# Where the gate product, the next token tile's split and the weight conversion stand in a fused attention and two-layer MoE kernel

## The chip, the cores and the metric

The kernel runs on one core of one Trainium2 chip. The metric is the device time of one execution in microseconds (us). Three executions of the kernel before took 931.65, 932.81 and 933.22 us; the median is 932.81 us.

## The reference, cut to what matters

```python
# q, k, v: (4, 8, 576, 64)
kv  = einsum('bhsd,bhse->bhde', k, v)
o   = einsum('bhsd,bhde->bhse', q, kv)
x   = o / sqrt(mean(o*o, -1) + 1e-6) * g_norm      # to (2304 tokens, 512)
y   = (sigmoid(x @ w_gate) * (x @ w_val)) @ w_out  # 512 -> 1536 -> 512
out = softplus(y @ w_in2) @ w_out2                 # 512 -> 2048 -> 512
```

All is fp32. The kernel reaches that accuracy by splitting both operands of a product into a rounded part (HI) and a rest (LO) and adding three fp32r matmuls: HI by HI, HI by LO, LO by HI, with the weight first. So a product needs the LO half of its weight at its third matmul and the LO half of the data at its second.

## The kernel before, in words

**Order.** The program is written out by hand. Each engine works through its own queue in the order in which the Python code emits instructions, so the place of a call in the loop is its place in the queues of PE (TensorE), ACT (ScalarE), DVE (VectorE) and SP (DMA issue).

**Tiles and iterations.** The first layer has five token tiles (512, 512, 384, 384, 512 tokens) and 12 blocks of 128 hidden columns: 60 iterations n = (t, i). One iteration has three groups of 12 matmuls: `ffn1_mm` "g" (PSUM tile ps_g), `ffn1_mm` "v" (ps_v) and `ffn1_out` of the iteration before it (yacc). The second layer follows with 80 iterations (ps_h, oacc). ps_g and ps_v share the pool `mm`, which has two buffers. So the v product of iteration n+1 can only start when `gated` of iteration n has read ps_v, and the g product of n+1 when `sigmoid` of n has read ps_g.

**After the products.** `sigmoid` (L488, ACT) writes sg. `gated` multiplies sg by ps_v (L494, DVE) and rounds the result into ghl HI (L67, ACT); `gated_lo` writes ghl LO (L70, DVE). Before the change `gate_prev` and `gate_lo_prev` call these for the previous iteration, after the g product of this one.

**Weights.** Weights arrive as raw fp64 words in 18 items of 1 MB for the first layer, each with a block of SBUF of its own, and 16 for the second. Item numbers go gate/value 0, gate/value 1, out 0 and 1, gate/value 2, gate/value 3, out 2 and 3, and so on: iteration 1 needs item 1 for g and v and item 2 for its out product, iteration 2 needs item 3, iteration 3 items 4 and 5. An item is converted on the chip: `conv_a` (two ACT instructions, L141 and L143), `conv_b` (two DVE, L150 and L153), `conv_h` (one ACT, L67) and `conv_l` (one DVE, L70). `conv_step` makes one step of each for successive items; `conv_to(m)` repeats it until m items are done. `A_LIM` and `L_END` say how far it goes in each iteration; the steps of an iteration are spread over three places.

**Attention.** Token tile 0 is prepared before the loop (L370 transposes it, `xt_split` at L381 and L382 splits it), interleaved with the first three quarters of g(0) and the conversion of weight 0 in two halves (`early_*`). Tile 1 is prepared during iterations 2 to 8 of the loop: `kv_mm` (L258), `qt_mm` (L320), `o_mm` (L332), `o_scale` (L364), `xt_mm` (L370). Later tiles come during the tile ahead of them, in 28 pieces of one head pair: `q_trans` (transpose L422, then the split of hl), `po_mm`, `po_evac`, `ss_mm`, `rms_root`, `rms_scale`. A table of places says where: "A", "B", "C" are slots behind the g, v and out products on PE, and "a", "b", "c", "bg" and "late" the matching slots for ACT and DVE.

**Scratch.** Before the loop the last seven weight blocks hold attention data (k, v, q rows, squares, the output rows `ON`). Their weight loads come when the data is used up.

```python
    def mm3(ps, lhs, rhs, start, stop):                    # L63
        for n, (a, b) in enumerate(PASSES): ...
    def gated(t, i):
        nc.vector.tensor_tensor(out=sg, in0=sg, in1=chain.pop(("v", t, i)), op=ALU.mult)   # L494
        split_hi(ghl[:, HI], sg)                           # L67
    def conv_step():
        na, nb = n_a[0], n_b[0]
        if n_h[0] < nb: conv_h()
        if na < min(n_load[0], a_lim[0]): conv_a()
        if nb < na: conv_b()
        if n_l[0] < n_h[0]: conv_l()
    def x_split(u):                                        # x: one buffer for all tiles
        for hp in range(NP):
            split(x_tile(u)[:, hp, HI, :n], x_t[u][:, hp, LO, :n], of_t[u][:, hp, :n])
```

Of the kernel before, what the change touches and what calls it, by code (L numbers as in the profile page):

```python
# [29 lines left out]
def attention_moe_moe_kernel(ctx: ExitStack, tc: tile.TileContext, q, k, v, g_norm,  # L30
                             w_gate, w_val, w_out, w_in2, w_out2, out):
    nc = tc.nc
# [4 lines left out]
    P = 128  # L37
# [172 lines left out]

    SCR = [n for n in range(n_first - 7, n_first)]
    KV, QROWS, QT, SQ, KVF, ON = 0, 5, (7, 8), 9, 10, (12, 13)
    scr_t = {}

    def scratch(gen, j, name):
# [94 lines left out]
    def half(u, j, hp, name):  # L312
        return scratch(u, j, name)[:, hp % 2 * 512:(hp % 2 + 1) * 512]
# [25 lines left out]
    def o_square(u, hp):  # L339
# [5 lines left out]
        nc.scalar.activation(out=sq, in_=ps, func=ACTF.Square)  # L345
        nc.vector.tensor_reduce(out=ms_t[u, 0][:, hp], in_=heads(sq), op=ALU.add, axis=AXIS.X)

    def on_rows(u, hp):
        return half(u, ON[hp // 2], hp, "on").rearrange("p (n m) -> p n m", m=P)


    def o_keep(u, hp):
# [13 lines left out]
    def xt_mm(u, hp, pool):  # L366
        ps = pool[0].tile([P, 512], F32, tag=pool[1], name="xT")
        on = on_rows(u, hp)
        for n in range(NS):
            nc.tensor.transpose(ps[:, n * P:(n + 1) * P], on[:, n], ident)  # L370
        at_ps["xT", u, hp] = ps
# [275 lines left out]
    def early_l(j):  # L647
        split_lo(early["w"][:, j, LO], early[j][:, :, 0].bitcast(F32), early["w"][:, j, HI])
# [66 lines left out]
    xt_mm(0, 2, ACC)  # L715
    a_root(3)
    a_scale(3)
    nc.scalar.preload_act_table_set("sigmoid_and_others")
    xt_split(0, 2)
    ffn1_mm(0, 0, "g", (1,))  # L720
    early_b(1)
    xt_mm(0, 3, ACC)
    early_h(1)
    xt_split(0, 3)
    early_l(1)
    ffn1_mm(0, 0, "g", (2,))
    a_lim[0] = 2
    conv_a()
    conv_b()
    for part in (0, 1, 2, 3, "rest"):  # L730
        load_kv(1, part)
# [20 lines left out]
    def at_mm(places, mm_fs, evac_fs):  # L752
        for (n, c), f, g in zip(places, mm_fs, evac_fs):
# [1 line left out]
            at_place(n, c.lower(), g)  # L755

    hps = range(NP)
    at_mm(((2, "A"), (2, "B"), (2, "C"), (3, "A")), [call(kv_mm, 1, h) for h in hps], [call(kv_evac, 1, h) for h in hps])
    at_mm(((3, "B"), (3, "C"), (4, "A"), (4, "B")), [call(qt_mm, 1, h, ATP) for h in hps],
          [call(qt_evac, 1, h) for h in hps])  # L760
    at_mm(((4, "C"), (5, "A"), (5, "B"), (5, "C")), [call(o_mm, 1, h, ATP) for h in hps],
          [lambda h=h: (o_square(1, h), o_keep(1, h)) for h in hps])
    at_place(6, "bg", call(o_root, 1, slice(0, NP)))
    at_place(6, "late", call(o_scale, 1, 0), call(o_scale, 1, 1))
    at_place(7, "bg", call(o_scale, 1, 2), call(o_scale, 1, 3))
    at_place(7, "late", call(kvb_split))
    at_mm(((7, "A"), (7, "B"), (7, "C"), (8, "A")), [call(xt_mm, 1, h, ATP) for h in hps],
          [call(xt_keep, 1, h) for h in hps])
    for n, c, m in ((3, "late", 2), (4, "late", 1), (5, "late", 2), (8, "bg", 2)):
        at_place(n, c, *[load_item] * m)  # L770

    for u in range(2, NT1):
        j = (u - 1) * F1 + (0 if u > 2 else 1)
        ps = pieces(u)
        for n, p in enumerate(ps):
            b, m = p[0], p[3]
            if (b > ps[n - 1][0] if n else b > (TILES1[u][0] - 1) // S):
                at_place(j - 1, "bg", call(load_kv, b, "rest"), call(load_kv, b, 0), call(load_kv, b, 1))
                for part, c in ((2, "b"), (3, "c")):
                    at_place(j, c, call(load_kv, b, part))  # L780
                for hp, (d, c) in enumerate(((0, "B"), (0, "C"), (1, "A"), (1, "B"))):
                    at_place(j + d, c, call(kv_mm, b, hp))
                    work[j + d, c.lower()] = [call(kv_evac, b, hp)] + work.get((j + d, c.lower()), [])
                j += 2
            at_place(j - 1, "bg", call(load_q, u, p))
            step = 2 if m <= 160 else 1
            for h0 in range(0, NP, step):
                hh = range(h0, h0 + step)
                at_place(j, "a", *[call(q_trans, u, p, h) for h in hh])
                at_place(j, "B", *[call(po_mm, u, p, h) for h in hh])  # L790
                at_place(j, "b", *[call(po_evac, u, p, h) for h in hh])
                j += 1
                at_place(j, "A", *[call(ss_mm, u, p, h) for h in hh])
                at_place(j, "a", *[call(ss_evac, u, p, h) for h in hh])
            at_place(j, "bg", call(rms_root, u, p))
            if n + 1 < len(ps) and TILES1[u - 1][1] < 512 and m > 160:
                when = ((1, "bg"), (2, "bg"), (3, "bg"), (4, "bg"))
            else:
                when = ((1, "bg"), (1, "late"), (2, "bg"), (2, "late"))
            for h, (d, c) in enumerate(when):  # L800
                at_place(j + d, c, call(rms_scale, u, p, slice(h, h + 1)))
            if u == 3 and n == 0:
                j += 1


    A_LIM = (4, 6, 7, 9, 10, 12, 13, 15, 16, 18, 18, 18)
    L_END = (3, 5, 6, 8, 9, 11, 12, 14, 15, 17, 18, 18)

    def conv_target(n):
        i = n - (n1 - F1)  # L810
# [13 lines left out]
    for n in range(len(its) + LAG2):  # L824
        ph, t, i = its[n] if n < len(its) else (0, 0, 0)
        prev = its[n - 1] if 0 < n <= len(its) else (0, 0, 0)

        def run(place):
            for f in work.pop((n, place), ()):
                f()  # L830

        def gate_prev():
            if prev[0] == 1:
                gated(*prev[1:])

        def gate_lo_prev():
            if prev[0] == 1:
                gated_lo(*prev[1:])

        if ph == 1:  # L840
            done = n_l[0]
            step = max(0, conv_target(n) - done)
            ffn1_mm(t, i, "g", range(3 if n == 0 else 0, KD))
            run("A")
            gate_prev()
            run("a")
            gate_lo_prev()
            if n:
                conv_to(done + (step + 2) // 3)
            sigmoid(t, i)  # L850
            run("bg")
            if t == NT1 - 1 and i < 2:
                y_split(0, 2 * i)
                y_split(0, 2 * i + 1)
            ffn1_mm(t, i, "v")
            run("B")
            conv_to(done + (2 * step + 2) // 3)
            run("b")
            conv_to(done + step)
        elif ph == 2:  # L860
            if n == n1:
                gate_prev()
                gate_lo_prev()
                xs.close()
                g2pool = ctx.enter_context(tc.tile_pool(name="g2pool", bufs=3))
                epool = ctx.enter_context(tc.tile_pool(name="epool", bufs=2))
                nc.scalar.preload_act_table_set("natural_log_exp_and_others")
            ffn2_mm(t, i)
            if prev[0] == 2:
                soft_sum(*prev[1:])  # L870
            if n_l[0] < len(items) and i % 2 == 0:
                a_lim[0] = len(items)
                conv_step()
            if t + 1 < NT2:
                if i == 10:
                    y_load(t + 1)
                if F2 - KD <= i:
                    y_split(t + 1, i - F2 + KD)
            soft_exp(t, i)
            if prev[0] == 2:  # L880
                soft_hi(*prev[1:])
            soft_ln(t, i)
            if prev[0] == 2:
                soft_lo(*prev[1:])
        elif n == len(its):
            soft_sum(*prev[1:])
            soft_hi(*prev[1:])
            soft_lo(*prev[1:])
        if prev[0] == 1:
            ffn1_out(*prev[1:])  # L890
        if n >= LAG2 and its[n - LAG2][0] == 2:
            ffn2_out(*its[n - LAG2][1:])
        run("C")
        run("c")
        run("late")
        if ph == 1 and t == NT1 - 1:
            n_free[0] = i + 1 + i // 2
            prefetch()
        if ph == 1 and i == F1 - 1 and t + 1 < NT1:
            x_split(t + 1)  # L900
            if t + 1 == NT1 - 1:
                at.close()
                y0pool = ctx.enter_context(tc.tile_pool(name="y0pool", bufs=1, side="right"))
        if ph == 1 and t == NT1 - 2 and i == F1 - 3:
            y_load(0)
# [31 lines left out]
```

## Time and profile before

| what | value |
|---|---|
| median of three executions | 932.81 us |
| the profiled execution's own time | 931.42 us |
| span of its instructions | 929.6 us |
| mean granted TensorE clock | 0.992 of full speed |
| PE busy | 907.6 us, 98% |
| DVE busy | 548.4 us, 59% |
| ACT busy | 457.3 us, 49% |

Times in the trace count from the start of the span. The profiled execution is 1.8 us longer than its span and 1.4 us shorter than the median. A bracket behind a row of a timeline gives the time for which the engine stood idle ahead of it and what ended that. Instructions that follow one another on an engine overlap a little in the record, so a sum over rows uses the distance of their starts.

### The profile page before, as it was taken

To read this page: it belongs to the slowest core of one execution; us is meant where nothing else is said; L and a number is where in the kernel's file an instruction comes from. 1 tells how busy PE (TensorE), PEld (TensorE's weight loads), DVE (VectorE), ACT (ScalarE), POOL (GpSimd) and SP (SyncE) were. 2 spreads that over 40 slices of the span, in tenths; PEclk is the share of its full clock that TensorE was granted. 3 is DMA by queue.
4 is the path that set the end of the run, shared out by engine and by line. 5 is a ranking of instruction groups with operands and counts; after the bars stand their busy time and mean duration, and the time that the engine had idled before them with its cause. 6 is when DMAs were issued, how large, how long until landed. Compare 5 with 4: busy or idle time off the path is not lost.

```text
span 929.6 us, 11913 instructions
## 1 busy us (share of the span) xinstructions
PE 907.6 (98%) x4653; PEld 780.9 (84%) x4653; DVE 548.4 (59%) x908; ACT 457.3 (49%) x791; POOL 1.6 (0%) x8
## 2 busy tenths in 40 slices
PE   8699989999999999999999999999999999999998
PEld 6477778878899999999888878888888999888886
DVE  4755784343555534575475688765556666566554
ACT  4646773332345343543565576554454454555443
POOL 0000000000000000000000000000000000000000
PEclk9799999999999999999999999999999999999999
DMA  9982130330011302002556301011002002000001
GB/s 307 281 285 95 51 103 0 103 76 7 1 57 52 78 6 71 10 24 61 200 195 212 110 27 46 1 42 38 1 1 80 1 1 81 1 0 35 1 1 45
DMA packets 73960, 64.73 MB, mean 70 GB/s; under 512 B 33200, under 2 KB 64944, under 8 KB 73904
## 3 DMA queue, kind: packets, MB, share of 16 engines
q1 hardware_dynamic: 72672, 63.33, 21.8%
q10 hardware_dynamic: 1232, 0.66, 0.3%
q8 instruction: 36, 0.59, 0.2%
q14 instruction: 20, 0.16, 0.1%
HBM read 54.53 MB, written 9.44 MB: 69 GB/s over the span
## 4 chain that ended last, share of the span: by engine, by line
PE 88%; DVE 5%; DMA 3%; SPq 2%; issue 1%; ACT 1%
PE oacc L63 21%; PE ps_h L63 21%; PE yacc L63 15%; PE ps_v L63 15%; PE ps_g L63 14%; DMA kv_raw<-in_k_dram 2%; DVE w_raw L150 1%; DVE w L70 1%; SPq L130 1%; PE kv_ps L258 1%; PE po L63 1%; DVE w L153 1%; DMA kv_raw<-in_q_dram 0%; DMA w_raw<-in_moe_w_out_dram 0%; DMA q_raw<-in_q_dram 0%
## 5 line engine op out<-in xcount | busy, mean ns | idle before, releaser
L63 PE MATMUL oacc<-w,ghl 128*128 128x512 f32 x864 | 210.7, 391 | 0.7 <-DVE ghl L70 0.7
L63 PEld LDWEIGHTS oacc<-w,ghl 128*128 128x128 f32 x864 | 161.4, 188 | 34.1 <-DVE ghl L70 1.9
L63 PE MATMUL ps_v<-x,w 128*128 128x512 f32 (+1 forms) x720 | 163.6, 376 | 8.3 <-DVE sg L494 8.2
L63 PE MATMUL ps_g<-x,w 128*128 128x512 f32 (+1 forms) x720 | 161.2, 371 | 2.9 <-ACT x L381 2.2
L63 PE MATMUL yacc<-ghl,w 128*128 128x512 f32 (+1 forms) x720 | 159.6, 370 | 0.0
L63 PEld LDWEIGHTS ps_v<-x,w 128*128 128x128 f32 x720 | 132.3, 192 | 27.6 <-DVE sg L494 10.0
L63 PEld LDWEIGHTS ps_g<-x,w 128*128 128x128 f32 x720 | 130.8, 188 | 21.9 <-ACT x L381 2.8
L63 PEld LDWEIGHTS yacc<-ghl,w 128*128 128x128 f32 x720 | 129.8, 188 | 16.6
L560 ACT ACTIVATE e<-ps_h 128x512 f32<-128x512 f32 (+1 forms) x80 | 44.4, 555 | 180.7 <-PE ps_h L63 171.5
L63 PE MATMUL ps_h<-y,w 128*128 128x512 f32 (+1 forms) x576 | 128.3, 372 | 0.0
L63 PEld LDWEIGHTS ps_h<-y,w 128*128 128x128 f32 x576 | 106.2, 188 | 16.4
L569 DVE TENSOR_SCALAR u<-e 128x512 f32<-128x512 f32 (+1 forms) x80 | 32.0, 399 | 133.1 <-ACT e L561 133.0
L67 ACT CAST ghl<-sg 128x512 fp32r<-128x512 f32 (+1 forms) x60 | 34.6, 577 | 103.2 <-DVE sg L494 103.0
L63 PE MATMUL ps_h<-y_odd,w 128*128 128x512 f32 (+1 forms) x384 | 82.4, 363 | 0.0
L63 PEld LDWEIGHTS ps_h<-y_odd,w 128*128 128x128 f32 x384 | 70.2, 188 | 8.9
L494 DVE TENSOR_TENSOR sg<-sg,ps_v 128x512 f32<-128x512 f32 (+1 forms) x60 | 37.7, 629 | 46.2 <-PE ps_v L63 44.4
L488 ACT ACTIVATE sg<-ps_g 128x512 f32<-128x512 f32 (+1 forms) x60 | 33.3, 555 | 39.5 <-PE ps_g L63 39.4
L578 DVE TENSOR_TENSOR e<-e,u 128x512 f32<-128x512 f32 (+1 forms) x80 | 51.1, 638 | 2.8
L571 DVE SCALAR_TENSOR_TENSOR e<-ps_h,e 128x512 f32<-128x512 f32 (+1 forms) x80 | 51.0, 638 | 2.8
L70 DVE TENSOR_TENSOR ghl<-sg,ghl 128x512 fp32r<-128x512 f32 (+1 forms) x60 | 38.1, 636 | 23.5 <-ACT ghl L67 23.3
L70 DVE TENSOR_TENSOR ghl<-e,ghl 128x512 fp32r<-128x512 f32 (+1 forms) x80 | 50.3, 628 | 0.7 <-ACT ghl L67 0.7
L570 ACT ACTIVATE ln<-u 128x512 f32<-128x512 f32 (+1 forms) x80 | 47.2, 591 | 6.8 <-DVE u L569 6.0
(97 smaller groups left out, 774.1 us busy)
## 6 DMA issues: line engine op xcount, KB each, us to landing
w_raw<-in_moe_w_out_dram SPq DMA_DIRECT2D x28, 512.0 KB, 4.5
w_raw<-in_moe_w_in_dram SPq DMA_DIRECT2D x16, 512.0 KB, 4.9
w_raw<-in_moe_w_gate_dram SPq DMA_DIRECT2D x12, 512.0 KB, 5.8
w_raw<-in_moe_w_val_dram SPq DMA_DIRECT2D x12, 512.0 KB, 7.5
out_dram<-ob SPq DMA_DIRECT2D x17, 256.0 KB, 2.5
kv_raw<-in_k_dram SPq DMA_DIRECT2D x16, 256.0 KB, 3.7
kv_raw<-in_v_dram SPq DMA_DIRECT2D x14, 256.0 KB, 4.0
y_dram<-ys SPq DMA_DIRECT2D x6, 512.0 KB, 2.8
```

What stands on the lines that cost most here:

```text
L63: nc.tensor.matmul(out=ps, lhsT=lhs(a), rhs=rhs(b), start=start and n == 0, stop=stop and n == 2)
L67: nc.scalar.copy(out=hi, in_=src)
L70: nc.vector.tensor_tensor(out=lo, in0=src, in1=hi.bitcast(F32), op=ALU.subtract)
L130: nc.sync.dma_start(out=t, in_=unit(w, f))
L150: nc.vector.scalar_tensor_tensor(out=lo, in0=hi, scalar=3, in1=lo, op0=ALU.logical_shift_left, op1=ALU.bitwise_or)
L488: nc.scalar.activation(out=sg, in_=chain.pop(("g", t, i)), func=ACTF.Sigmoid)
L494: nc.vector.tensor_tensor(out=sg, in0=sg, in1=chain.pop(("v", t, i)), op=ALU.mult)
L560: nc.scalar.activation(out=e, in_=ps, func=ACTF.Abs)
L569: nc.vector.tensor_scalar(out=u, in0=e, scalar1=1.0, scalar2=None, op0=ALU.add)
L570: nc.scalar.activation(out=ln, in_=u, func=ACTF.Ln)
L571: nc.vector.scalar_tensor_tensor(out=e, in0=chain.pop(("p", t, i)), scalar=0.0, in1=e, op0=ALU.max, op1=ALU.add)
L578: nc.vector.tensor_tensor(out=e, in0=e, in1=u, op=ALU.subtract)
```

## The change

The gate product of an iteration is finished in that iteration: `sigmoid` comes straight after the g product, `gated` and `gated_lo` after the v product. The conversion is spread over two places, ahead of the v product and behind `gated_lo`, and iterations 0 and 1 each finish one item fewer (`L_END`), though iteration 0 begins one step more. `x_split` of the next token tile moves ahead of `gated` in the last iteration of a tile. Before the loop the sigmoid table is loaded behind the conversion `conv_a` of item 1, which itself moves ahead of `early_l(1)`. The output rows `on` live in the tile `of`, so six scratch blocks do, item 11 is loaded before the loop, and later loads come earlier. Most places of tile 1's attention move forward by one, and so do those of `rms_scale`.

```diff
-    SCR = [n for n in range(n_first - 7, n_first)]
-    KV, QROWS, QT, SQ, KVF, ON = 0, 5, (7, 8), 9, 10, (12, 13)
+    SCR = [n for n in range(n_first - 6, n_first)]
+    KV, QROWS, QT, SQ, KVF = 0, 5, (7, 8), 9, 10
...
     def on_rows(u, hp):
-        return half(u, ON[hp // 2], hp, "on").rearrange("p (n m) -> p n m", m=P)
+        return of_tile(u)[:, hp].rearrange("p (n m) -> p n m", m=P)
...
     a_root(3)
     a_scale(3)
-    nc.scalar.preload_act_table_set("sigmoid_and_others")
     xt_split(0, 2)
     ffn1_mm(0, 0, "g", (1,))
     early_b(1)
+    a_lim[0] = 2
     xt_mm(0, 3, ACC)
     early_h(1)
     xt_split(0, 3)
+    conv_a()
     early_l(1)
     ffn1_mm(0, 0, "g", (2,))
-    a_lim[0] = 2
-    conv_a()
+    nc.scalar.preload_act_table_set("sigmoid_and_others")
     conv_b()
...
-    at_mm(((2, "A"), (2, "B"), (2, "C"), (3, "A")), [call(kv_mm, 1, h) for h in hps], ...
-    at_mm(((3, "B"), (3, "C"), (4, "A"), (4, "B")), [call(qt_mm, 1, h, ATP) for h in hps],
-    at_mm(((4, "C"), (5, "A"), (5, "B"), (5, "C")), [call(o_mm, 1, h, ATP) for h in hps],
+    at_mm(((1, "C"), (2, "A"), (2, "B"), (2, "C")), [call(kv_mm, 1, h) for h in hps], ...
+    at_mm(((3, "A"), (3, "B"), (3, "C"), (4, "A")), [call(qt_mm, 1, h, ATP) for h in hps],
+    at_mm(((4, "B"), (4, "C"), (5, "A"), (5, "B")), [call(o_mm, 1, h, ATP) for h in hps],
+    at_place(5, "late", call(kvb_split))
     at_place(6, "bg", call(o_root, 1, slice(0, NP)))
-    at_place(6, "late", call(o_scale, 1, 0), call(o_scale, 1, 1))
-    at_place(7, "bg", call(o_scale, 1, 2), call(o_scale, 1, 3))
-    at_place(7, "late", call(kvb_split))
+    at_place(6, "b", call(o_scale, 1, 0))
+    at_place(6, "c", call(o_scale, 1, 1))
+    at_place(7, "bg", call(o_scale, 1, 2))
+    at_place(7, "b", call(o_scale, 1, 3))
-    for n, c, m in ((3, "late", 2), (4, "late", 1), (5, "late", 2), (8, "bg", 2)):
+    for n, c, m in ((2, "late", 2), (3, "late", 1), (4, "late", 1), (5, "late", 1), (8, "bg", 1)):
         at_place(n, c, *[load_item] * m)
...
-                when = ((1, "bg"), (1, "late"), (2, "bg"), (2, "late"))
+                when = ((0, "late"), (1, "bg"), (1, "late"), (2, "bg"))
             for h, (d, c) in enumerate(when):
                 at_place(j + d, c, call(rms_scale, u, p, slice(h, h + 1)))
...
     A_LIM = (4, 6, 7, 9, 10, 12, 13, 15, 16, 18, 18, 18)
-    L_END = (3, 5, 6, 8, 9, 11, 12, 14, 15, 17, 18, 18)
+    L_END = (2, 4, 6, 8, 9, 11, 12, 14, 15, 17, 18, 18)
...
             ffn1_mm(t, i, "g", range(3 if n == 0 else 0, KD))
             run("A")
-            gate_prev()
+            sigmoid(t, i)
             run("a")
-            gate_lo_prev()
-            if n:
-                conv_to(done + (step + 2) // 3)
-            sigmoid(t, i)
             run("bg")
+            conv_to(done + (step + 1) // 2)
             if t == NT1 - 1 and i < 2:
                 y_split(0, 2 * i)
                 y_split(0, 2 * i + 1)
             ffn1_mm(t, i, "v")
             run("B")
-            conv_to(done + (2 * step + 2) // 3)
+            if i == F1 - 1 and t + 1 < NT1:
+                x_split(t + 1)
+            gated(t, i)
             run("b")
+            gated_lo(t, i)
             conv_to(done + step)
+            if n == 0:
+                conv_step()
         elif ph == 2:
             if n == n1:
-                gate_prev()
-                gate_lo_prev()
                 xs.close()
...
         if ph == 1 and i == F1 - 1 and t + 1 < NT1:
-            x_split(t + 1)
             if t + 1 == NT1 - 1:
```

## Rows read from the trace of the kernel before

**Rows 1.** Page, part 1: busy time, share of the span, instructions.

```profile
PE 907.6 (98%) x4653; PEld 780.9 (84%) x4653; DVE 548.4 (59%) x908; ACT 457.3 (49%) x791; POOL 1.6 (0%) x8
```

**Rows 2.** Waits of PE over the whole span: us in total, times, longest.

```profile
PE ps_v L63 <- DVE sg L494: 8.2, 4, 4.9
PE xT L370 <- DVE on L364: 2.5, 2, 1.3
```

**Rows 3.** Timeline of PE, 24 to 56 us: start, us, engine, line, operation, idle before.

```profile
24.48 0.66 PE L370 MATMUL xT<-kvf,on 128*128 128x128 f32 x4 [1.23 <-DVE on L364]
...
28.82 2.00 PE L63 MATMUL ps_g<-x,w 128*128 128x512 f32 x3 [1.85 <-ACT x L381]
30.62 4.53 PE L63 MATMUL ps_v<-x,w 128*128 128x512 f32 x12
...
43.27 5.08 PE L63 MATMUL ps_v<-x,w 128*128 128x512 f32 x12 [4.91 <-DVE sg L494]
48.19 2.91 PE L63 MATMUL yacc<-ghl,w 128*128 128x512 f32 x12
50.94 2.88 PE L63 MATMUL ps_g<-x,w 128*128 128x512 f32 x12
53.75 0.95 PE L258 MATMUL kv_ps<-kv_raw 128*64 128x64 f32 x20
54.62 3.01 PE L63 MATMUL ps_v<-x,w 128*128 128x512 f32 x12
```

**Rows 4.** Windows: busy us of PE, PEld, DVE, ACT, POOL; PE clock; DMA.

```profile
28.00:34.00 6.00, 5.18 (x11) 3.76 (x12) 3.81 (x4) 3.99 (x6) 0.00 (x0) 0.50 1.06 371
...
38.00:43.00 5.00, 0.36 (x2) 0.00 (x0) 4.97 (x5) 1.73 (x2) 0.00 (x0) 0.79 0.72 140
...
103.00:106.00 3.00, 3.00 (x14) 2.42 (x14) 1.92 (x2) 3.00 (x4) 0.00 (x0) 1.00 0.94 294
```

**Rows 5.** Timeline of ACT, 23 to 31 us.

```profile
23.41 1.28 ACT L718 ACT_TABLE_LOAD   x1
24.71 0.69 ACT L381 ACTIVATE x<-xT,g_col 128x512 fp32r<-128x512 f32 x1
...
28.67 1.15 ACT L141 ACTIVATE w_raw<-w_raw 128x1024 f32<-128x1024 f32 x1
```

**Rows 6.** Timeline of DVE, 25 to 44 us.

```profile
25.43 0.75 DVE L382 SCALAR_TENSOR_TENSOR x<-xT,g_col,x 128x512 fp32r<-128x512 f32 x1 [1.00 <-ACT x L381]
...
40.26 1.23 DVE L153 SCALAR_TENSOR_TENSOR w<-w_raw 128x1024 uint32<-128x1024 uint32 x1
41.40 1.22 DVE L70 TENSOR_TENSOR w<-w,w 128x1024 fp32r<-128x1024 f32 x1
42.54 0.68 DVE L494 TENSOR_TENSOR sg<-sg,ps_v 128x512 f32<-128x512 f32 x1
```

**Rows 7.** Groups of DVE and ACT over the span: busy us, mean ns.

```profile
L150 DVE SCALAR_TENSOR_TENSOR w_raw<-w_raw 128x1024 uint32<-128x1024 uint32 x33 | 40.3, 1220 | 3.9 <-ACT w_raw L143 3.8
...
L141 ACT ACTIVATE w_raw<-w_raw 128x1024 f32<-128x1024 f32 x33 | 38.3, 1160 | 0.0
...
L67 ACT CAST w<-w 128x1024 fp32r<-128x1024 f32 x33 | 34.5, 1047 | 10.5 <-DVE w L153 10.0 <-ACT w_raw L143 0.3
```

**Rows 8.** DMA issues, 32.9 to 35 us: KB each, us to landing.

```profile
kv_raw<-in_v_dram SPq DMA_DIRECT2D x1, 128.0 KB, 6.1
```

**Rows 9.** Timeline of PE, 100 to 125 us.

```profile
102.76 3.06 PE L63 MATMUL ps_v<-x,w 128*128 128x512 f32 x12 [2.12 <-DVE sg L494]
...
124.20 3.06 PE L63 MATMUL ps_v<-x,w 128*128 128x512 f32 x12 [0.96 <-DVE sg L494]
```

**Rows 10.** Timeline of all engines, 273 to 275 us, one q piece.

```profile
273.86 0.49 ACT L488 ACTIVATE sg<-ps_g 128x384 f32<-128x384 f32 x1
273.98 0.33 DVE L70 TENSOR_TENSOR hl<-qT,hl 128x160 fp32r<-128x160 f32 x1 [0.45 <-ACT hl L67]
...
274.36 0.79 PE L63 MATMUL po<-hl,kvb 128*128 128x160 f32 x6
```

More of the change, by code (lines that the diff above doesn't have):

```diff
@@ L757, in attention_moe_moe_kernel @@
     hps = range(NP)
-    at_mm(((2, "A"), (2, "B"), (2, "C"), (3, "A")), [call(kv_mm, 1, h) for h in hps], [call(kv_evac, 1, h) for h in hps])
-    at_mm(((3, "B"), (3, "C"), (4, "A"), (4, "B")), [call(qt_mm, 1, h, ATP) for h in hps],
+    at_mm(((1, "C"), (2, "A"), (2, "B"), (2, "C")), [call(kv_mm, 1, h) for h in hps], [call(kv_evac, 1, h) for h in hps])
+    at_mm(((3, "A"), (3, "B"), (3, "C"), (4, "A")), [call(qt_mm, 1, h, ATP) for h in hps],
           [call(qt_evac, 1, h) for h in hps])
-    at_mm(((4, "C"), (5, "A"), (5, "B"), (5, "C")), [call(o_mm, 1, h, ATP) for h in hps],
+    at_mm(((4, "B"), (4, "C"), (5, "A"), (5, "B")), [call(o_mm, 1, h, ATP) for h in hps],
           [lambda h=h: (o_square(1, h), o_keep(1, h)) for h in hps])
+    at_place(5, "late", call(kvb_split))
     at_place(6, "bg", call(o_root, 1, slice(0, NP)))
-    at_place(6, "late", call(o_scale, 1, 0), call(o_scale, 1, 1))
-    at_place(7, "bg", call(o_scale, 1, 2), call(o_scale, 1, 3))
-    at_place(7, "late", call(kvb_split))
+    at_place(6, "b", call(o_scale, 1, 0))
+    at_place(6, "c", call(o_scale, 1, 1))
+    at_place(7, "bg", call(o_scale, 1, 2))
+    at_place(7, "b", call(o_scale, 1, 3))
     at_mm(((7, "A"), (7, "B"), (7, "C"), (8, "A")), [call(xt_mm, 1, h, ATP) for h in hps],
           [call(xt_keep, 1, h) for h in hps])
-    for n, c, m in ((3, "late", 2), (4, "late", 1), (5, "late", 2), (8, "bg", 2)):
+    for n, c, m in ((2, "late", 2), (3, "late", 1), (4, "late", 1), (5, "late", 1), (8, "bg", 1)):
         at_place(n, c, *[load_item] * m)
@@ L830, in run @@
                 f()
[L832 to L838, printed above, removed]
         if ph == 1:
```

## The prediction

> **What bounds the kernel now.** I read the busy shares first: PE is busy for 907.6 of 929.6 us [rows 1], so at most 22 us are there to be won by waiting less. The list of PE's waits comes next: the largest is ps_v behind the gate product (L494), 8.2 us in four waits, 4.9 in one of them; then xT behind L364, 2.5 us in two [rows 2]. The timeline of PE says where: 1.23, 1.85 and 4.91 us before 44 us [rows 3], and 2.12, 0.96 and one xT wait of 1.3 between 100 and 125 us [rows 2, 9]. All of it lies in the first 130 us. After that PE goes from matmul to matmul, and the change can win nothing there, only lose.
>
> The wait of 4.91 us has its cause in DVE's queue. DVE is busy for 4.97 of the 5 us from 38 to 43 [rows 4]: before the gate product of iteration 0 it converts items 2 and 3 and finishes item 2 (L153 at 40.26, L70 at 41.40), and L494 follows without a gap at 42.54 [rows 6]. v(1) needs the ps_v buffer that L494 frees. The clock adds to that. It is 0.50 of full speed, the level of 1.2 GHz, from 28 to 34 us, and it falls again during the long wait (0.79 on average from 38 to 43 us) [rows 4]. So v(0) takes 4.53 us and v(1) 5.08, where 3.01 is usual [rows 3].
>
> **The change, part by part.** Durations are those of the rows. An instruction that follows another on DVE or ACT starts some 0.1 us before the recorded end of the first (L153 1.23 long, L70 1.14 later [rows 6]); so I use 2.4 us for `conv_b`, 1.15 for `conv_l`, 2.05 for `conv_a`, 0.95 for `conv_h` [rows 6, 7], 0.6 for the gate product or its LO half, 2.75 for 12 matmuls of 512 columns and 0.87 for a `kv_mm` [rows 3].
>
> *The table load.* It stands from 23.41 to 24.69 ahead of `xt_split` of head pair 2 [rows 5], and DVE stood idle for 1.00 us behind that [rows 6]. Without it the chain `xt_split`(2), `early_b`, `early_h`, `xt_split`(3), `conv_a`(1) comes 1.1 us earlier: DVE can start 0.1 us before the recorded end of the instruction ahead. So `conv_a`(1) starts at 27.57 in place of 28.67 [rows 5]. The wait of 1.85 remains, 1.1 us earlier. The load then runs behind `conv_a`(1), from 29.6 to 30.9, while ACT waits for g(0) anyway; sigmoid(0) ends at 31.5, and `conv_h`(1) waits for `conv_b`(1) until 32.3. It costs nothing there; without that cover it would cost its 1.28.
>
> The next instruction starts 0.02 us after the load ends [rows 5]. The Trainium skill (ScalarE: Activation LUTs, What ACT_TABLE_LOAD costs) adds about 1.38 us of drain to a load of 1.283. By that, `conv_h`(1) would come 0.5 us later and the sum below be 0.5 less; the row shows the load but no drain, and I take the row.
>
> *The queues of iterations 0 to 2.* I walk the new order. `conv_b`(1) ends at 32.3, `conv_h`(1) at 33.35, `conv_l`(1) at 34.6, L494 of iteration 0 at 35.2 (v(0) ends near 33.9 if the clock is low as before), its HI half behind `conv_a`(2) at 35.9, its LO half at 36.6. DVE then goes on without a pause worth counting: `conv_b`(2) to 39.05, `conv_b`(3) to 41.4, `conv_l`(2) to 42.6, L494 of iteration 1 to 43.2, LO half 43.85 to 44.5, `conv_b`(4) to 46.9, `conv_l`(3) to 48.0.
>
> PE: g(1) needs `conv_l`(1) at its third matmul and ends at 36.9. v(1) finds ps_v free since 35.2 and ends at 39.7. The 4.91 is gone. But out(0) needs weight item 2, formerly ready early. Its HI half comes at 40.15, its LO half at 42.6: PE waits 0.5 and then 2.0 us, and out(0) ends at 44.9. `kv_mm`, now at (1, "C"), ends at 45.8; its last rows were issued by 35 us and take 6.1 to land [rows 8], so they are there. g(2) has the LO half of item 3 at 48.0: another 1.8 us, end at 50.3. With the second `kv_mm`, v(2) starts at 51.2.
>
> Before, v(2) started at 54.62 with one `kv_mm` done instead of two [rows 3]; that is 55.5 for equal work. **First term: 55.5 - 51.2 = 4.3 us.** What is late next is DVE's conversion chain; the table load's 1.1 us is inside this term.
>
> From v(2) on the walk finds PE never waiting: items 4 to 7 are ready some 3 to 8 us before their products, and L494 comes within 1 us of the end of its v product, where PE leaves it an out and a g product, 5.5 us, before it wants the buffer.
>
> *Later waits.* Three of ps_v (8.2 - 4.91 = 3.3) and one of xT (2.5 - 1.23 = 1.3) remain after 56 us [rows 2, 3]. The first kind goes because the later half of the conversion is now behind L494; in the tightest place, iteration 5, L494 ends 1.7 us before v(6) wants the buffer, in iterations 7 and 9 about 1.5. The xT wait goes because `o_scale` moves up to its own slots; the last transpose keeps only 0.3 us of margin behind `xt_keep`. **Second term: 4.6 us**, with 3.6 if that margin and one more give way by half a microsecond each.
>
> *Parts at nothing.* `x_split` ahead of L494 at four tile ends: four LO halves and the product take about 3.9 us of DVE behind v, and PE gives 5.5 (out and g of 512 columns; the mean of four 384-column pieces is shorter on both sides). Without that cover it costs the excess, 4 times. `on` in `of`: same instructions, other addresses; no reader of the old data is later than the new writer. Item 11 loaded before the loop adds 1 MB to a busy DMA stretch, but it stands behind items 6 to 10 in SP's queue and nothing wants it before 85 us. The later loads pass nothing: SP's queue is empty there. `rms_scale` is DVE work with a tile end as its due time.
>
> *Sum.* 4.3 + 4.6 = 8.9 us. The span goes from 929.6 to 920.7, the profiled execution's time from 931.42 to 922.5. The median of the runs is 1.4 above that execution; from it, 932.81 - 8.9 = **923.9 us**.
>
> **The rivals.**
>
> *The clock falls in the new waits.* Between 39.7 and 48 us PE now waits 0.5, 2.0 and 1.8 us with little work between. For it: the clock fell in the waits before 28 and before 43 us [rows 4]. Against: it stayed at 1.00 behind the wait of 2.12 us at 100 us [rows 4, 9]. Price: what v(1) lost, 5.08 - 3.01 = 2 us [rows 3], in part hidden by the second wait. Time 924.9 to 925.9.
>
> *Waits for weights in place of waits for buffers.* L494 now stands in DVE's queue until v is done, with half of the conversion behind it. If DVE loses enough there, items come late in iterations 3 to 10 and the second term does not come, and an iteration or two pays a `conv_l` wait of 1.15. Against: the margins of 3 us and more. Time 932.81 - 4.3 = 928.5.
>
> *No change within the bound.* Both together: 4.3 - 2 = 2.3 from the first term, given back by two weight waits of 1.15: 932.8.
>
> *Slower: sigmoid ahead of the q split.* In the loop of tiles 1 to 3, sigmoid moved ahead of "a", so the split of q waits for the end of g and 0.49 us more on ACT. In the tightest place before, hl of the second head pair ended at 274.31 and po started at 274.36 [rows 10]. There are 20 iterations with such a split and 7 with a table switch in them. Price if everything is exposed: 20 x 0.49 + 7 x 1.28 = 18.8 us, time 942.7. It decides from 10.8 us on (8.9 and the bound), a good half of that. Against: the second pair's matmuls come 0.3 us behind the first's (half of the 0.79), ACT's copies of ss formerly waited for PE anyway, and the table switch runs while PE is in out and g. I find 0.1 us of margin at the worst place and no wait.
>
> **How the numbers follow.** A difference of 0.2%, 1.9 us, is about what a measurement of this kernel can tell from none. Chances: forecast (923.9, within about 1.5) 0.63; clock 0.18; weights 0.11; no change 0.04; slower 0.04. So faster 0.92, same 0.04, slower 0.04. The range reaches down to 921.5: 1.2 us for a base as low as the fastest of the three runs (931.65), and 1.2 for waits of out(0) and g(2) that come out half as long as walked in one place. It reaches up to 928.0, past the clock rival and nearly to the weights rival, since a walk by hand over three queues leaves out small delays.
>
> **What would show it.** Right: no wait of ps_v on L494 in the list; v(1) with no wait and 3.0 us long; in its place waits of out(0) and g(2) on L70 w, together 4 to 4.5 us, between 39 and 48 us; v(2) near 51; no xT wait at 115 us; po without a wait; the stretch from 130 us to the end as long as before. A clock of 0.5 between 43 and 51 us is the clock rival; waits on L70 w after 52 us the weights rival; waits of po on hl the slower one. A first term under 2 us would prove my walk of DVE's queue wrong.

## The result and the profile after

The changed kernel takes 924.73 us (median of four executions, 924.35 to 925.94) against 932.88 for the kernel before in the same comparison: ratio 0.9917, 95% interval 0.99 to 0.9934. That is 8.15 us less by the medians. The profiled execution takes 924.62 us, its span went from 929.6 to 922.8 us: 6.8 less. The two differ because the profiled execution of before lay 1.5 us under its median and that of after at its median.

The list of PE's waits comes first, as before [rows 2].

```profile
PE ps_g L63 <- DVE w L70: 2.1, 3, 1.0
PE ps_g L63 <- ACT x L382: 1.9, 1, 1.9
PE yacc L63 <- DVE w L70: 1.7, 1, 1.7
PE ps_v L63 <- DVE sg L495: 1.2, 1, 1.2
PE xT L371 <- DVE of L365: 1.2, 1, 1.2
```

The 8.2 us behind the gate product are down to 1.2, in one wait. One xT wait of two is left, the one before the loop. New are waits for weights: `w L70` is the LO half of a converted item. The timeline of PE from 27 to 52 us shows the first of them; it answers to [rows 3].

```profile
27.75 0.50 PE L63 MATMUL ps_g<-x,w 128*128 128x512 f32 x1 [1.86 <-ACT x L382]
...
29.11 4.50 PE L63 MATMUL ps_v<-x,w 128*128 128x512 f32 x12
...
37.14 2.88 PE L63 MATMUL ps_v<-x,w 128*128 128x512 f32 x12
40.31 0.73 PE L63 MATMUL yacc<-ghl,w 128*128 128x512 f32 x2 [0.29 <-ACT w L67]
42.70 4.14 PE L63 MATMUL yacc<-ghl,w 128*128 128x512 f32 x10 [1.65 <-DVE w L70]
46.77 0.95 PE L258 MATMUL kv_ps<-kv_raw 128*64 128x64 f32 x20
47.65 3.13 PE L63 MATMUL ps_g<-x,w 128*128 128x512 f32 x12
...
51.58 3.01 PE L63 MATMUL ps_v<-x,w 128*128 128x512 f32 x12
```

v(1) waits for nothing and takes 2.88 us where it had 5.08. out(0) splits into 2 and 10 matmuls: the third needs the LO half of item 2. Its ten matmuls take 4.14 us, not 2.6, because the clock fell in the wait. The windows (busy of the engines, then granted clock, DMA share and GB/s) show that:

```profile
38.00:42.00 4.00, 2.75 (x11) 1.62 (x10) 3.97 (x4) 3.37 (x5) 0.00 (x0) 1.00 0.73 147
42.00:46.00 4.00, 3.31 (x9) 2.64 (x10) 3.28 (x5) 3.06 (x5) 0.00 (x0) 0.66 0.87 217
```

Five later places of PE's timeline changed sign or size. In the first, g(6) takes 3.29 us in place of the usual 2.88: it waits inside the group. The next two are listed waits for weights in g(8) and g(10). The fourth, a po group that takes 1.19 us in place of 0.79, waits inside the group as well. The last is a wait of v(52) for the gate product of iteration 51.

```profile
92.58 3.29 PE L63 MATMUL ps_g<-x,w 128*128 128x512 f32 x12
...
112.37 2.57 PE L63 MATMUL ps_g<-x,w 128*128 128x512 f32 x10 [1.02 <-DVE w L70]
...
129.97 2.60 PE L63 MATMUL ps_g<-x,w 128*128 128x512 f32 x10 [0.51 <-DVE w L70]
...
286.62 1.19 PE L63 MATMUL po<-hl,kvb 128*128 128x160 f32 x6
...
456.62 3.03 PE L63 MATMUL ps_v<-x,w 128*128 128x512 f32 x12 [1.24 <-DVE sg L495]
```

Most useful for the whole study was a ledger: the time at which v(n) starts, read from PE's timeline for every n. Where two kernels keep their distance, nothing differs; a step shows a wait with its full price, restart included. h(63) is the fourth product of the second layer; behind it every distance stays to the end. Labels are those of the experiments below.

| start of | before | changed | changed, again | e1 | e2 | e4 | e5 | e8 | e11 |
|---|---|---|---|---|---|---|---|---|---|
| xT | 24.48 | 24.51 | 24.69 | 24.27 | 24.62 | 24.26 | 24.62 | 25.03 | 24.13 |
| v(0) | 30.62 | 29.11 | 29.74 | 30.42 | 30.77 | 28.87 | 29.22 | 30.08 | 28.80 |
| v(2) | 54.62 | 51.58 | 53.34 | 54.05 | 50.83 | 50.53 | 50.87 | 52.12 | 50.43 |
| v(2), from xT on | 30.14 | 27.07 | 28.65 | 29.78 | 26.21 | 26.27 | 26.25 | 27.09 | 26.30 |
| v(12) | 157.50 | 148.73 | 150.47 | 151.16 | 154.49 | 148.42 | 156.76 | 149.24 | 146.91 |
| v(29) | 300.62 | 292.25 | 293.99 | 294.71 | 297.62 | 291.96 | 299.88 | 292.79 | 290.03 |
| v(52) | 463.59 | 456.62 | 458.36 | 459.07 | 460.58 | 457.59 | 464.53 | 455.75 | 453.00 |
| h(63) | 540.04 | 533.19 | 534.92 | 535.63 | 537.04 | 535.34 | 541.12 | 532.17 | 529.42 |

The row xT is the group of transposes that waits 1.23 us before the loop [rows 3]. No edit touches what stands ahead of it, so its start tells how late the first loads came in that profile. v(0) does not serve for that, since its start also depends on the table load and on the clock.

(Ahead of v(2) there is one `kv_mm`, 0.88 us, fewer in before and e2 than in the others.) So the change had won 8.77 us at v(12), nearly all of the forecast 8.9, and gave back 0.4 before v(29) and 1.55 by the iteration behind v(52).

### The profile page after: what moved, and what is told of

It is laid out like the page before. It is cut to its first block, busy times and chain, and to the rows that moved or that the text cites. A ratio compares the mean times of both kernels' runs of the same rounds, so it can differ in the third digit from the quotient of the medians.

```text
span 922.8 us, 11897 instructions
## 1 busy us (share of the span) xinstructions
PE 905.3 (98%) x4653; PEld 779.5 (84%) x4653; DVE 549.6 (60%) x908; ACT 453.3 (49%) x791; POOL 1.6 (0%) x8
## 4 chain that ended last, share of the span: by engine, by line
PE 90%; DVE 4%; DMA 2%; ACT 2%; SPq 1%; issue 1%; ACTq 0%; DVEq 0%
PE oacc L63 21%; PE ps_h L63 21%; PE yacc L63 15%; PE ps_g L63 15%; PE ps_v L63 15%; PE kv_ps L258 1%; DVE w_raw L150 1%; PE po L63 1%; DVE w L70 1%; DVE w L153 1%; DMA w_raw<-in_moe_w_gate_dram 1%; DMA kv_raw<-in_k_dram 1%; SPq L416 1%; PE o_rows L332 1%; PE qt L320 0%
## 5 line engine op out<-in xcount | busy, mean ns | idle before, releaser
L63 PE MATMUL yacc<-ghl,w 128*128 128x512 f32 (+1 forms) x720 | 161.6, 373 | 1.9 <-DVE w L70 1.7
L63 PE MATMUL ps_v<-x,w 128*128 128x512 f32 (+1 forms) x720 | 161.1, 372 | 1.2 <-DVE sg L495 1.2
L63 PEld LDWEIGHTS ps_g<-x,w 128*128 128x128 f32 x720 | 130.1, 188 | 23.6 <-DVE w L70 4.1
L561 ACT ACTIVATE e<-ps_h 128x512 f32<-128x512 f32 (+1 forms) x80 | 44.4, 555 | 180.6 <-PE ps_h L63 171.5
L495 DVE TENSOR_TENSOR sg<-sg,ps_v 128x512 f32<-128x512 f32 (+1 forms) x60 | 37.8, 630 | 50.4 <-PE ps_v L63 45.3
L70 DVE TENSOR_TENSOR ghl<-sg,ghl 128x512 fp32r<-128x512 f32 (+1 forms) x60 | 38.1, 636 | 21.7 <-ACT ghl L67 21.4
L70 DVE TENSOR_TENSOR w<-w,w 128x1024 fp32r<-128x1024 f32 x33 | 40.2, 1219 | 18.2 <-ACT w L67 18.1
L70 DVE TENSOR_TENSOR ghl<-e,ghl 128x512 fp32r<-128x512 f32 (+1 forms) x80 | 50.3, 628 | 0.7 <-ACT ghl L67 0.7
```

What stands on the lines that cost most here:

```text
L63: nc.tensor.matmul(out=ps, lhsT=lhs(a), rhs=rhs(b), start=start and n == 0, stop=stop and n == 2)
L70: nc.vector.tensor_tensor(out=lo, in0=src, in1=hi.bitcast(F32), op=ALU.subtract)
L561: nc.scalar.activation(out=e, in_=ps, func=ACTF.Abs)
```

## The experiments

Medians and ratios to the kernel before, each against executions of that kernel from the same series:

| label | edit | us | ratio (95% interval) |
|---|---|---|---|
| e1_table_back | changed, table load at its old place | 925.98 | 0.9934 (0.9918 to 0.9949) |
| e2_lend_alone | before, new L_END alone | 928.33 | 0.9956 (0.9942 to 0.997) |
| e3_conv_behind | changed, last tile converts behind the gate product | 925.14 | 0.9923 (0.9909 to 0.9937) |
| e4_lo_first | changed, `conv_l` ahead of `conv_b` | 929.06 | 0.9961 (0.9945 to 0.9976) |
| e5_gate_next | changed, gate product in the next iteration | 934.45 | 1.0021 (1.001 to 1.0032) |
| e6_scale_old | changed, old places of `rms_scale` | 925.76 | 0.9927 (0.9915 to 0.994) |
| e8_conv51 | changed, iteration 51 alone converts behind | 923.63 | 0.9909 (0.9895 to 0.9924) |
| e9_table_fill | e1 with idle matmuls in the waits | 925.83 | 0.993 (0.9916 to 0.9943) |
| after_again | changed | 924.85 | 0.9924 (0.9909 to 0.9938) |
| e10_scale_moved | changed, one `rms_scale` moved | 924.65 | 0.9924 (0.9909 to 0.9939) |
| e11_best | three edits together | 923.42 | 0.9908 (0.9889 to 0.9926) |

**What made the first term: L_END alone.**

```diff
 (kernel before)
-    L_END = (3, 5, 6, 8, 9, ...
+    L_END = (2, 4, 6, 8, 9, ...
```

> The kernel before with the new L_END alone (iterations 0 and 1 finish one weight item fewer); gate product, table load and places as before. Theory A, the first term comes from what DVE converts ahead of the gate product, not from the iteration in which the gate product is written: a walk of the old queues gives L494 of iteration 0 at 36.4, no wait of v(1), out(0) waiting for item 2 until 43.7, g(2) for item 3 until 47.3, v(2) with one kv_mm done at 50.3 in place of 54.6; the waits between 100 and 125 us stay; time 932.9 - 4.3 = 928.6 us. Theory B, the gate product's own iteration is what removes the wait of v(1): at most 1 us, 932.

Measured: 928.33 us, 3.5 under the 931.87 of before in that series; v(2) at 50.83, 3.8 earlier. Its PE timeline:

```profile
43.93 2.57 PE L63 MATMUL yacc<-ghl,w 128*128 128x512 f32 x10 [1.66 <-DVE w L70]
...
50.83 3.01 PE L63 MATMUL ps_v<-x,w 128*128 128x512 f32 x12
...
98.29 4.54 PE L63 MATMUL ps_v<-x,w 128*128 128x512 f32 x12 [2.12 <-DVE sg L494]
```

Theory A holds. For equal work (one `kv_mm` more) this is 51.7, as good as the changed kernel's 51.58. Two numbers in a table remove the wait of 4.91 us; the rest of the change adds nothing by v(2) on balance. That balance has two sides, as e5 and e1 show below: the gate product's new place costs 0.8 us there, and the table load's new place gives 1.1. The waits from 98 us on stay, and here the clock fell in one of them (v(6) takes 4.54 us).

**What made the second term: the gate product's place.**

```diff
 (changed kernel)
             run("A")
+            if prev[0] == 1:
+                gated(*prev[1:])
+            run("a")
+            if prev[0] == 1:
+                gated_lo(*prev[1:])
             sigmoid(t, i)
-            run("a")
...
-            gated(t, i)
             run("b")
-            gated_lo(t, i)
...
```

> The changed kernel with the gate product put back into the next iteration (after its g product, sigmoid behind gated_lo), all else as changed. Theory: the second term came from the gate product's place; waits of v on it return in iterations 5 to 9, 2 to 5 us together by the starts, v(12) starts at 151 to 154 in place of 148.7; the wait at v(52) and the 0.4 us at 287 us go; startup up to v(2) as in the changed kernel within 0.5 us; time 925 to 928. Rival, the second term came from the earlier places of kv, qt, o and o_scale alone: v(12) within 0.5 of 148.7, no ps_v waits, time 922.8.

Measured: 934.45 us, slower than before. v(2) stands 0.7 us earlier than in the changed kernel (0.82 from xT on, where at most 0.5 was expected) and v(12) 8.0 us later. PE's waits in between:

```profile
99.28 3.06 PE L63 MATMUL ps_v<-x,w 128*128 128x512 f32 x12 [3.02 <-DVE sg L495]
...
121.31 3.02 PE L63 MATMUL ps_v<-x,w 128*128 128x512 f32 x12 [1.72 <-DVE sg L495]
...
140.31 3.01 PE L63 MATMUL ps_v<-x,w 128*128 128x512 f32 x12 [1.57 <-DVE sg L495]
```

The theory was right in direction and too small: not 2 to 5 but 8.7 us from v(2) to v(12). The rest of the change is no gain by itself: with the old place of the gate product this stretch takes 3.9 us more than in the kernel before at equal work (105.9 against 102.0). Which part of the rest costs that, the earlier places or the conversion in two parts, no run shows. The 0.8 us by which v(2) is early are what the new place costs in the first iterations. There PE waits for the LO half of item 3, the last row of both fences (the first of this kernel, the second of the changed one). In the changed kernel the gate product of iteration 1, its LO half and a wait of 0.69 us between them stand ahead of it on DVE. From xT on it ends at 22.51 us here and at 23.64 there.

```profile
45.91 1.22 DVE L70 TENSOR_TENSOR w<-w,w 128x1024 fp32r<-128x1024 f32 x1
```

```profile
43.92 0.69 DVE L70 TENSOR_TENSOR ghl<-sg,ghl 128x512 fp32r<-128x512 f32 x1 [0.69 <-ACT ghl L67]
...
46.93 1.22 DVE L70 TENSOR_TENSOR w<-w,w 128x1024 fp32r<-128x1024 f32 x1
```

Behind v(12) one part of the expectation held and one missed. The 0.4 us before v(29) stays away: from v(12) to v(51) this kernel keeps its distance to the one before within 0.3 us. The wait at v(52) does not: v(51) still starts 0.45 us ahead of the kernel before, v(53) 1.10 behind, and v(52) again waits 1.24 us for L495. That is the same 1.55 us as in the changed kernel, so this wait does not hang on the iteration in which the gate product is written; what it hangs on is shown below.

**The table load.**

```diff
     a_root(3)
     a_scale(3)
+    nc.scalar.preload_act_table_set("sigmoid_and_others")
     xt_split(0, 2)
...
     ffn1_mm(0, 0, "g", (2,))
-    nc.scalar.preload_act_table_set("sigmoid_and_others")
```

> The changed kernel with the sigmoid table load put back ahead of xt_split of head pair 2. Theory: the load costs its 1.28 us of ACT there and shifts the whole chain to g(2) by 1.1 us; v(2) starts near 52.7 in place of 51.6 and the time is 925.8 us (924.7 + 1.1). Rival, a drain of 1.38 us belongs to a load: some 2.5 us later, 927.2. Rival, the chain is bound elsewhere and the load is covered: 924.7.

Measured: 925.98 us, 1.1 to 1.3 more than the changed kernel's medians. The ledger is less plain: v(1) comes 0.9 us later, v(2) 2.47 (1.14 and 2.71 from xT on). That is near the number of the drain rival, but its rows deny it: ACT goes on 0.02 us after the load, and PE's ten matmuls of g(2) run at half clock.

```profile
23.20 1.28 ACT L719 ACT_TABLE_LOAD   x1
24.50 0.69 ACT L382 ACTIVATE x<-xT,g_col 128x512 fp32r<-128x512 f32 x1
```

```profile
43.60 2.55 PE L63 MATMUL yacc<-ghl,w 128*128 128x512 f32 x10 [1.65 <-DVE w L70]
...
49.10 4.14 PE L63 MATMUL ps_g<-x,w 128*128 128x512 f32 x10 [1.42 <-DVE w L70]
```

In the changed kernel's profile the clock fell in out(0), here in g(2). To tell the clock from the load, the next run keeps PE busy in the two waits:

```diff
 (kernel e1)
+    def fill(m):                       # zeros into a spare PSUM tile, m times 512 columns
+        ...
+            if n == 2:
+                fill(8)
             ffn1_mm(t, i, "g", ...
...
+        if n == 1:
+            fill(8)
         if prev[0] == 1:
             ffn1_out(*prev[1:])
```

> The kernel with the table load put back, and 8 matmuls on zeros (512 columns, some 1.75 us) ahead of out(0) and 8 ahead of g(2), where PE waits for weights anyway; they add work and no result uses them. Theory: of the 2.47 us by which v(2) came later there, 0.9 are the later chain and the rest is the clock, which fell to half in g(2); with PE kept busy it does not fall, the ten matmuls of g(2) take 2.6 us in place of 4.14 and v(2) starts near 52.5 in place of 54.05. Rival, g(2) is slow for another reason: v(2) at 54 or later by the filler's length.

```profile
47.54 2.11 PE L830 MATMUL fill<-kvb 128*128 128x512 f32 x8
49.49 2.88 PE L63 MATMUL ps_g<-x,w 128*128 128x512 f32 x12
```

g(2) runs at full clock. The first loads came 0.56 later in this profile; from xT on v(2) starts at 28.35 us against 29.78 in e1. So what e1 lost beyond the table load is the half clock of g(2). That the idle matmuls kept the clock up is not shown: it also held in a profile without them (e8, below), and by the medians (925.83 against 925.98 us) they gain nothing. The changed kernel itself, profiled again, has its fall where e1 has it:

> The changed kernel once more, on the chip of the next two runs, as the base they are compared with: 924.7 us, with v(2) 22.0 to 22.5 us behind v(0) whatever the first loads shift.

```profile
42.89 2.55 PE L63 MATMUL yacc<-ghl,w 128*128 128x512 f32 x10 [1.67 <-DVE w L70]
...
48.39 4.14 PE L63 MATMUL ps_g<-x,w 128*128 128x512 f32 x10 [1.42 <-DVE w L70]
```

Here v(2) stands 23.6 us behind v(0), not 22.0 to 22.5: the expectation missed. One kernel, and 1.6 us between two profiles (28.65 against 27.07 from xT on), by where the clock falls. The kernel of e8 (below) has the same start and the same two waits, and in its profile the clock fell in neither place:

```profile
43.25 2.56 PE L63 MATMUL yacc<-ghl,w 128*128 128x512 f32 x10 [1.65 <-DVE w L70]
...
48.75 2.56 PE L63 MATMUL ps_g<-x,w 128*128 128x512 f32 x10 [1.40 <-DVE w L70]
```

Its v(2) starts at 27.09 from xT on. So a fall in out(0) costs nothing by v(2): 4.14 - 2.56 = 1.6 us are lost, but g(2) then finds item 3 ready and does not wait. A fall in g(2) costs 1.56 us, for nothing hides it. With the fall in g(2) on both sides, e1 against the changed kernel profiled again, the table load's old place costs 1.13 us at v(2) and 1.11 at v(12): the theory's 1.1, and it stays.

**The wait at v(52).** DVE's timeline of the changed kernel shows why the gate product of iteration 51 is late:

```profile
449.95 1.23 DVE L150 SCALAR_TENSOR_TENSOR w_raw<-w_raw 128x1024 uint32<-128x1024 uint32 x1 [6.00 <-ACT w_raw L143]
...
452.35 1.22 DVE L150 SCALAR_TENSOR_TENSOR w_raw<-w_raw 128x1024 uint32<-128x1024 uint32 x1
...
454.75 1.22 DVE L70 TENSOR_TENSOR w<-w,w 128x1024 fp32r<-128x1024 f32 x1
455.88 0.68 DVE L495 TENSOR_TENSOR sg<-sg,ps_v 128x512 f32<-128x512 f32 x1
```

v(51) is done near 449.9, but the first item of the second layer takes two steps of the conversion, all ahead of the product (the half that goes there is rounded up, and of one item that is the whole), and these begin only when ACT has done its part behind sigmoid. In e5 the product is written an iteration later, but again behind the two steps, and ACT again starts them behind sigmoid. In the kernel before, ACT starts them ahead of it (451.51 against 457.20 us) and v(52) waits for nothing. So the cause is where the conversion stands, and the product is only what comes late by it. First all of the last tile was moved:

```diff
             run("bg")
-            conv_to(done + (step + 1) // 2)
+            if t < NT1 - 1:
+                conv_to(done + (step + 1) // 2)
```

> The changed kernel, but in the last tile of the first layer all of the conversion stands behind the gate product. Theory: the new wait of v(52) at 456.6 us comes from the conversion of the first second-layer item ahead of the gate product of iteration 51; it goes, worth 1.5 us by the starts: 923.2 us. Rival, the wait is set by the landing of the weights or by ACT: it stays or moves to a weight wait, 924.7.

Measured: 925.14 us, no gain. The rival named no right cause, though: the wait at v(52) is gone and v(59) starts 1.56 us earlier, and all of it is lost again between the second and the fourth product of the second layer:

```profile
526.62 3.06 PE L63 MATMUL ps_h<-y,w 128*128 128x512 f32 x12 [0.53 <-DVE e L572]
...
530.80 2.58 PE L63 MATMUL oacc<-w,ghl 128*128 128x512 f32 x10 [0.28 <-DVE ghl L70]
```

What is late is ACT's half of the conversion: it now stands behind the last gate product, ahead of the softplus chain.

```profile
516.04 0.62 ACT L67 CAST ghl<-sg 128x512 fp32r<-128x512 f32 x1 [2.85 <-DVE sg L495]
...
524.09 0.62 ACT L561 ACTIVATE e<-ps_h 128x512 f32<-128x512 f32 x1
```

Between these two rows ACT works without a pause, on two items and a table load. The softplus (L561) begins 6.3 us behind the start of its product at 517.77; in the changed kernel it is 3.3 us (519.33 to 522.61), and DVE waits 0.97 us for it here. So the next run moved one iteration only:

```diff
-            conv_to(done + (step + 1) // 2)
+            if (t, i) != (NT1 - 1, 3):
+                conv_to(done + (step + 1) // 2)
```

> The changed kernel with the conversion behind the gate product in iteration 51 alone, where two steps are needed to finish the first item of the second layer. Theory: v(52) starts 1.5 us earlier and, since the later items are converted as early as in the changed kernel, nothing is given back at the start of the second layer: time 923.2. Rival, as when all iterations of that tile were changed, the gain is lost again near 530 us: 924.7.

Measured: 923.63 us. In the ledger v(51) stands 0.53 behind the changed kernel's (first loads) and v(53) 1.02 ahead: 1.55 won, and kept to the end. The theory holds. The medians alone, 1.1 us apart with overlapping intervals, would not show it.

**The 0.4 us before v(29).** In the changed kernel the timelines of DVE and ACT, one after the other, read:

```profile
283.73 1.14 DVE L467 RECIPROCAL ms<-ms 128x160 f32<-128x160 f32 x1
284.91 0.39 DVE L468 SCALAR_TENSOR_TENSOR of<-of,g_col,ms 128x160 f32<-128x160 f32 x1
285.21 0.34 DVE L423 STREAM_TRANSPOSE qT<-q_raw 128x160 f32<-128x160 f32 x1
```

```profile
285.59 0.33 ACT L67 CAST hl<-qT 128x160 fp32r<-128x160 f32 x1 [0.46 <-DVE qT L423]
```

ACT waits for the transpose, not for the sigmoid. The first try put `rms_scale` of such pieces to its old places:

```diff
+            elif n + 1 < len(ps):
+                when = ((1, "bg"), (1, "late"), (2, "bg"), (2, "late"))
             else:
                 when = ((0, "late"), (1, "bg"), (1, "late"), (2, "bg"))
```

> The changed kernel with the old places of rms_scale, except behind the last piece of a tile. Theory: the 0.39 us lost at 287 us (v(29)) come from a reciprocal of 1.14 us that stands on DVE ahead of the transpose of q; it goes and v(29) starts at 291.9 in place of 292.25; time 924.3. Rival, the sigmoid ahead of the q split causes them: the loss stays, 924.7.

The step stayed (0.40 us between v(28) and v(29)), but the slot (1, "late"), which holds the reciprocal in question, is in both lists: the run decided nothing. The second try used `((0, "late"), (1, "bg"), (2, "bg"), (2, "late"))`:

> The changed kernel with the third rms_scale of a piece that is not the last of its tile moved from the late slot of the iteration after the root to the bg slot of the one behind it. The run with the old places left a reciprocal ahead of the transpose of q in iteration 28, so it decided nothing; this one takes it away. Theory, the reciprocal on DVE: the step of 0.39 us between v(28) and v(29) against the kernel before goes; 924.3. Rival, sigmoid ahead of the split on ACT: it stays.

```profile
285.22 0.55 DVE L70 TENSOR_TENSOR ghl<-sg,ghl 128x384 fp32r<-128x384 f32 x1
285.69 0.34 DVE L423 STREAM_TRANSPOSE qT<-q_raw 128x160 f32<-128x160 f32 x1
```

The transpose follows `gated_lo` at once, and the distance to the kernel before is 6.81 us at v(28) and at v(29) alike: the step is gone. The reciprocal on DVE made it. By the medians (924.65 against 924.85 in that series) 0.4 us can't be seen.

**The weight waits.**

```diff
     def conv_step():
...
-        if nb < na:
-            conv_b()
         if n_l[0] < n_h[0]:
             conv_l()
+        if nb < na:
+            conv_b()
```

> The changed kernel with conv_l ahead of conv_b in each conversion step, so the LO half of an item is finished before the next item is begun. Theory, DVE's order is what the weight waits hang on: item 2 is done at 41.5 in place of 42.7, item 3 at 47.3 in place of 48.1, the waits of g(8) at 112 and of g(10) at 130 us go; 1.0 + 1.3 + 0.7 = 3 us, time 921.7. Rival, ACT's HI half sets them: no change, 924.7. Rival, the gate product of iteration 1, now behind conv_b, becomes late and v waits for it: 924 to 926.

```profile
41.31 2.60 PE L63 MATMUL yacc<-ghl,w 128*128 128x512 f32 x10 [0.53 <-DVE w L70]
...
103.98 0.63 PE L371 MATMUL xT<-kvf,of 128*128 128x128 f32 x4 [1.40 <-DVE of L365]
...
115.01 0.66 PE L371 MATMUL xT<-kvf,of 128*128 128x128 f32 x4 [1.24 <-ACT of L392]
...
457.59 3.02 PE L63 MATMUL ps_v<-x,w 128*128 128x512 f32 x12 [2.50 <-DVE sg L495]
```

Measured: 929.06 us, 4.2 to 4.3 more than the changed kernel by the medians and 2.2 by the ledger's h(63); why its other executions take longer than the profiled one (926.77) isn't shown. At the places named it does what the theory said: v(2) 1.05 earlier (0.80 from xT on), no wait in g(8) and g(10). But `o_scale` and `xt_keep` come later and the transposes wait 1.40 and 1.24 us, and v(52) waits 2.50 in place of 1.24. Another 1.1 us go between h(61) and h(63), as in e3. None of the rivals had these.

**Together.** The LO half first in iterations 0 to 2 and 8 to 10 only, iteration 51 converted behind, one `rms_scale` moved:

```diff
     def conv_step():
...
+        if lo_first[0] and n_l[0] < n_h[0]:
+            conv_l()
         if nb < na:
             conv_b()
-        if n_l[0] < n_h[0]:
+        if not lo_first[0] and n_l[0] < n_h[0]:
             conv_l()
...
+        lo_first[0] = n < 3 or 8 <= n < 11
...
```

> The changed kernel with three edits together: conversion of iteration 51 behind the gate product; conv_l ahead of conv_b in iterations 0 to 2 and 8 to 10 alone, where it took weight waits away without touching the transposes of iterations 7 and 8; the moved rms_scale. Theory, the terms add: 1.05 at v(2), 0.7 at v(10), 0.4 at v(29), 1.5 at v(52); 3.6 us, time 921.1, faster than both kernels. Rival, the waits only move, as they did in the last tile: under 1 us, 924.

Measured: 923.42 us (920.78 to 924.43), 1.4 under the changed kernel in the same series. The profiled execution took 920.78, its span is 919.0 us, and its ledger has every term. Against the changed kernel's first profile v(2) is 1.15 us earlier (0.38 of it are first loads, there at xT already, so 0.77 for the expected 1.05); by v(12) 0.67 more is won, by v(29) 0.40, by v(53) 1.55. The other three executions took 2.1 to 3.7 us more than the profiled one; their mean granted clocks are lower, 0.996, 0.994 and 0.993 for 922.91, 923.93 and 924.43 us against 0.998, which fits a fall of the clock, but they have no trace, so its place isn't shown. It is faster than the kernel before; that it is faster than the changed kernel too is likely, but its interval (0.9889 to 0.9926) overlaps with the other's (0.9909 to 0.9938).

## Why the prediction was right

**The walk of the queues held.** `conv_l`(2) was to end at 42.6 and ended at 42.64, L494 of iteration 1 at 43.2 (43.24), `conv_l`(3) at 48.0 (48.15), v(2) was to start at 51.2 and started at 51.58. The first term came to 3.9 for the forecast 4.3. Its price was right and its reason wide: the walk credited the order as a whole, and e2 shows that the smaller L_END alone gives 3.9. The table load's 1.1 us, said to be inside the term, is there (e1), but the gate product's own place takes 0.8 back (e5), which the walk did not tell apart. On PE the walk ended out(0) at 44.9; it ended at 46.8 for the clock, and v(2) still came in time only because g(2) waits for item 3 until 48 us either way. Where the clock falls in g(2), v(2) is 1.6 us later.

**The second term** was 4.6 and came to 4.85 from v(2) to v(12) at equal work (102.0 against 97.15 us), by two errors that nearly cancelled. The old waits were worth more than the list says: v(6) waited 2.12 us in [rows 9], but started 5.15 us after g(6) where 2.72 is usual, 2.43 lost. By the starts all of them cost 6.8 us, and the group behind a wait is 0.1 to 0.2 us slower as well. Against that, the statement that items are ready 3 to 8 us ahead failed: g(6), g(8) and g(10) waited 0.41, 1.29 and 0.67 us by the starts for their LO halves (in e4, with the LO half first, all three are gone). The walk had followed items 4 to 7 and looked at DVE only for the gate product after that. `conv_step` puts `conv_b` of the next item ahead of `conv_l` of this one, so an item that is finished just in time is 2.4 us later than a count of items says.

**Parts at nothing.** Right, by the list of waits and the ledger: `x_split` ahead of the product (no wait at any of four tile ends), item 11, the rows in `of`, the table load's new place. Wrong: "from 130 us to the end as long as before". The step that failed there is the one not walked: iteration 51, where the conversion of second-layer weights begins. Its half ahead of the product is the whole of it, 1.55 us. The prediction also read that all waits lie in the first 130 us; two small ones do not, 0.20 us at 141 and 0.74 at 544 us in the kernel before.

**The number.** The median came within 0.8 us of the forecast, but that is kinder than the walk deserves. Its 8.9 us stand against 6.8 between the two profiles: the profiled execution was to take 922.5 and took 924.62. The prediction took it that the median would lie 1.4 us above the profiled execution again; after the change it lies 0.1 above. That is luck.

**The rivals.** The clock did fall in the new waits, as that rival had it, at a price of nothing or 1.6 us by v(2), by its place, for a forecast 1 to 2. The weights rival came in small, 2.4 us in three places. The slower rival's place was right and its mechanism wrong: of 20 splits one waited, 0.39 us, for a reciprocal on DVE and not for the sigmoid. The drain of 1.38 us behind a table load that the Trainium skill gives (ScalarE: Activation LUTs, What ACT_TABLE_LOAD costs) is seen nowhere: in the changed kernel, too, ACT goes on at once.

```profile
29.78 1.28 ACT L729 ACT_TABLE_LOAD   x1
31.07 0.60 ACT L489 ACTIVATE sg<-ps_g 128x512 f32<-128x512 f32 x1
```

## What to carry to other kernels

Write in-order queues out by hand where a stretch is tight: the starts and ends named above came within 0.4 us here except where the clock fell, and what failed were the iterations that weren't walked. Put a consumer that frees a scarce buffer directly behind its producer and move deferrable work behind it, unless that work is what the next product waits for (by v(2) the move cost 0.8 us here). Then look for the first iteration in which the deferrable work changes size. Compare two profiles by the start of every repeated product; it prices a wait with its restart and shows at once where a gain is given back.

## What was not expected of the hardware

The place where the TensorE clock falls is not fixed by the program. Seven profiles share the changed kernel's start (both of the changed kernel, e1, e3, e6, e8 and e10): out(0) waits 1.65 to 1.67 us for item 2, and g(2) 1.40 to 1.42 us for item 3 where out(0) was not slowed. The ten matmuls behind the wait were at half speed in out(0) in three of them (4.13 to 4.14 us in place of 2.56), in g(2) in three (3.95 to 4.14), and in e8 in neither. By v(2) the first costs nothing and the second 1.6 us. In the one profile with eight matmuls on zeros in each wait there is no fall, but e8 has none without them, so whether they help isn't shown.
